# The second product of a feed-forward block in matmuls of 512 columns, with the 64 columns left over computed transposed

## The chip, the cores and the metric

The kernel runs on one core of a Trainium2 chip, in one launch. The metric is the time of an execution on the device in microseconds (us); three runs of the kernel before the change have a median of 1082.9 us (1082.35 to 1083.52). In the profile, PE is the matrix engine, PEld its weight loads, DVE the vector engine, ACT the scalar engine, POOL the third elementwise engine, and SP the queue that issues most DMAs.

## The reference, cut to what matters

```python
xn = _layernorm(x)                                    # x = A_q: 2048 rows, 576 columns
h  = jnp.maximum(jnp.einsum("bsd,df->bsf", xn, w1), 0)   # w1: 576 x 4608
B  = jnp.einsum("bsf,fd->bsd", h, w2)                 # w2: 4608 x 576: the second product
out = x + A(xn, k, v, shift_k, ssm_k, ssm_D) + B      # A: a causal long convolution with gates
```

A shifts and gates k and v, convolves them along the 2048 rows with ssm_k, and multiplies by xn. The kernel computes that convolution as matmul transforms of two steps (64 by 32).

## The kernel before, in words

All matmuls of the two products take fp32r operands, and every operand is split into a high part and a low part (`hi` by a rounding copy on ACT, `lo` by a subtraction on DVE or POOL), so that a product is the sum of three: high by high, high by low, low by high.

**Feed-forward.** The 2048 rows are 16 tiles of 128 rows (`T`), four blocks `b` of four tiles (`BT`). The 4608 hidden columns are 12 chunks `ci` of 384, each of three groups `j` of 128 (`FT`). The program passes twice over the 12 chunks (24 chunk visits), the first time with blocks 0 and 1, the second with blocks 2 and 3: 48 pairs of a chunk and a block. For each pair:

- `mm1` (line 334), three times: 14 matmuls of 512 columns (the moving operand is the transposed x of the block, `xhi`, `xlo`, `xhl`; the stationary one 128 by 128 of w1) into a PSUM tile `psh` of which there are two. ACT writes `hh` (the rectified high part, line 339), DVE `ll` (the low part, line 340).
- `mm2` (line 358), once for each of the four row tiles: for each half of the 576 output columns (`NH` = 288), nine matmuls of 288 columns, stationary a 128 by 128 slice of `hh` or `ll`, moving a half of `h2` or `l2` (high and low w2). The sum lies in a PSUM tile `pso`, of which there are three, and DVE adds it to `acc` in SBUF (line 362 for block 0, which is scaled by `rstd`, line 366 else).

That is 72 matmuls of 288 columns for a pair in `mm2`, 3456 in the program, beside 2016 of 512 columns in `mm1`. Every matmul has its own weight load of 128 by 128.

The weights of the next chunk are loaded by SP (`load_w1`, `load_w2`, lines 282 and 294) into single buffers, and split during the second block of a chunk: ACT writes the high part (lines 306 and 315), POOL the low part (line 277).

**Order.** `drain(n)` issues `mm2` tiles of the previous pair between the `mm1` groups of the next one: one after j=0, one after j=1, two after j=2. `tick(cost)` counts matmul columns and, at a rate from the totals, lets the generator `conv()` issue a further piece of the convolution: its matmuls are of 288 columns (lines 398, 562, 700 and 701) and stand in pairs or threes among those of the products, into the three PSUM tiles `psf`. A scheduler then sets the final order of the instructions on each engine. SP issues DMAs in order; in the first 60 us these are the loads of x, of the weights, and the many small pieces of `ssm_k` (`kt`, line 421).

At the end, the last row tile is stored in two halves, each issued by the SP and ACT queues after its addition (line 370).

## Time and profile before

| | |
|---|---|
| three runs, median | 1082.9 us (1082.35 to 1083.52) |
| span of the profiled execution (the page gives no time for it beside the span) | 1084.4 us |
| PE busy | 1070.8 us, 99% of the span |
| PEld busy | 977.2 us |
| DVE, ACT, POOL busy | 732.5, 585.0, 261.9 us |
| mean granted TensorE clock | 0.997 |
| matmuls | 6537: 2016 in `mm1`, 3456 in `mm2`, 960 in the convolution, 80 transposes, 25 to begin with |

The busy time of a matmul in the profile is from its start to its modelled end, and matmuls overlap. What a matmul costs in a full stream is the distance from its start to the start of the next one. The chain of waits gives this for whole stretches: a row such as "3.57 PE pso L358 x27" is 27 matmuls in a row that set the pace for 3.57 us. The timeline gives single starts.

### The profile page before, as it was taken

What the parts mean: (1) busy time and instruction counts of PE and PEld (TensorE: products, weight loads), DVE (VectorE), ACT (ScalarE), POOL (GpSimd) and SP (SyncE); (2) the same over time, 40 slices, a digit from 0 to 9 for tenths busy, and PEclk for the clock granted to TensorE, in tenths of its full rate; (3) what the DMA queues carried; (4) which work ended last, traced back from release to release, by engine and by line L of the source; (5) the groups of instructions that cost most, each with busy time, mean ns of one, the idle gap of its engine ahead of it and who ended that gap; (6) DMA issues with size and microseconds to landing.
All of it is one profiled execution on the core that took longest, in us unless ns stands there. A gap on an engine that the chain in (4) does not pass through costs nothing.

```text
span 1084.4 us, 17301 instructions
## 1 busy us (share of the span) xinstructions
PE 1070.8 (99%) x6537; PEld 977.2 (90%) x6537; DVE 732.5 (68%) x1213; ACT 585.0 (54%) x1184; POOL 261.9 (24%) x218
## 2 busy tenths in 40 slices
PE   8999999999999999999999999999999999999998
PEld 5889899998999999999999999899999999999998
DVE  5423677949998777677666676666656666876774
ACT  4221587823443323333388787888788864543430
POOL 4131222412312322312213031211113032332410
PEclk9999999999999999999999999999999999999999
DMA  9950345664644525325564343434344227745524
GB/s 217 181 145 27 119 147 190 195 185 133 187 138 136 153 77 164 117 60 171 190 182 135 99 135 99 135 99 136 92 143 141 80 103 221 201 130 143 164 81 110
DMA packets 112255, 150.79 MB, mean 139 GB/s; under 512 B 45261, under 2 KB 62927, under 8 KB 112172
## 3 DMA queue, kind: packets, MB, share of 16 engines
q1 hardware_dynamic: 103884, 135.50, 42.0%
q0 software_dynamic: 7968, 13.44, 4.8%
q8 instruction: 52, 0.85, 0.3%
q10 hardware_dynamic: 320, 0.74, 0.3%
q14 instruction: 31, 0.25, 0.1%
HBM read 114.26 MB, written 35.39 MB: 138 GB/s over the span
## 4 chain that ended last, share of the span: by engine, by line
PE 90%; DMA 4%; SPq 2%; DVE 2%; ACT 1%; issue 1%; POOL 0%; ACTq 0%; DVEq 0%
PE pso L358 40%; PE psh L334 39%; PE psf L562 7%; PE psf L398 3%; DMA r<-in_w 3%; SPq L421 2%; PE psf L700 1%; PE psf L701 1%; DMA k-1_2414<-in_k 1%; DMA sk<-in_shift_k 0%; PE psf L269 0%; DVE lok L553 0%; POOL l L277 0%; DVE k L611 0%; DVE lox L553 0%
## 5 line engine op out<-in xcount | busy, mean ns | idle before, releaser
L277 POOL TENSOR_TENSOR l<-r,h 128x640 fp32r<-128x640 f32 (+1 forms) x144 | 224.4, 1563 | 621.8 <-ACT h L306 448.3
L358 PE MATMUL pso<-h,hh 128*128 128x288 f32 x1152 | 337.3, 295 | 3.7 <-ACT hh L339 2.7
L358 PE MATMUL pso<-l,hh 128*128 128x288 f32 x1152 | 338.5, 295 | 0.0
L358 PE MATMUL pso<-h,ll 128*128 128x288 f32 x1152 | 337.7, 295 | 0.0
L334 PE MATMUL psh<-xhi,h 128*128 128x512 f32 x576 | 226.5, 394 | 1.1 <-DVE ll L340 1.1
L334 PE MATMUL psh<-xlo,h 128*128 128x512 f32 x576 | 226.5, 393 | 0.0
L334 PE MATMUL psh<-xhi,l 128*128 128x512 f32 x576 | 225.8, 392 | 0.0
L358 PEld LDWEIGHTS pso<-h,hh 128*128 128x128 f32 x1152 | 215.8, 188 | 10.4 <-ACT hh L339 3.4
L358 PEld LDWEIGHTS pso<-l,hh 128*128 128x128 f32 x1152 | 216.3, 188 | 5.8
L358 PEld LDWEIGHTS pso<-h,ll 128*128 128x128 f32 x1152 | 216.0, 188 | 0.6
L366 DVE TENSOR_TENSOR acc<-pso,acc 128x288 f32<-128x288 f32 x288 | 128.6, 451 | 75.1 <-PE pso L358 72.1
L339 ACT ACTIVATE hh<-psh 128x512 fp32r<-128x512 f32 x144 | 85.6, 595 | 169.1 <-PE psh L334 168.2
L340 DVE SCALAR_TENSOR_TENSOR ll<-psh,hh 128x512 fp32r<-128x512 f32 x144 | 99.0, 687 | 109.8 <-ACT hh L339 109.5
L334 PEld LDWEIGHTS psh<-xhi,l 128*128 128x128 f32 x576 | 108.4, 188 | 20.3
L334 PEld LDWEIGHTS psh<-xhi,h 128*128 128x128 f32 x576 | 108.4, 188 | 17.1 <-DVE ll L340 1.4
L334 PEld LDWEIGHTS psh<-xlo,h 128*128 128x128 f32 x576 | 108.6, 188 | 15.5 <-DVE xlo L204 0.4
L315 ACT ACTIVATE h<-r 128x576 fp32r<-128x576 f32 x72 | 48.9, 682 | 73.4 <-DMA r<-in_w 46.9
L362 DVE SCALAR_TENSOR_TENSOR acc<-pso,rstd,acc 128x288 f32<-128x288 f32 x96 | 48.3, 512 | 27.5 <-PE pso L358 26.5
L392 DVE TENSOR_TENSOR ks<-kt,ks 64x288 fp32r<-64x288 f32 x64 | 57.6, 901 | 3.3 <-ACT ks L391 1.3
L399 ACT ACTIVATE zx<-psf 128x288 f32<-128x288 f32 x64 | 25.8, 407 | 59.3 <-PE psf L398 38.9
L334 PE MATMUL psh<-xhl,l 128*128 128x512 f32 x144 | 56.4, 392 | 0.0
L334 PE MATMUL psh<-xhl,h 128*128 128x512 f32 x144 | 56.2, 391 | 0.0
(109 smaller groups left out, 1451.2 us busy)
## 6 DMA issues: line engine op xcount, KB each, us to landing
r<-in_w SPq DMA_DIRECT2D x24, 864.0 KB, 5.3
r<-in_w SPq DMA_DIRECT2D x23, 768.0 KB, 6.1
zk<-zk SPq DMA_DIRECT2D x32, 288.0 KB, 2.5
zx<-zx SPq DMA_DIRECT2D x32, 288.0 KB, 2.6
ztk<-zk SPq DMA_DIRECT2D x32, 288.0 KB, 3.0
ztx<-zx SPq DMA_DIRECT2D x32, 288.0 KB, 2.8
zy<-vo SPq DMA_DIRECT2D x32, 288.0 KB, 2.1
zo<-zy SPq DMA_DIRECT2D x32, 288.0 KB, 3.0
```

Of the source, the lines that this page charges most:

```text
L277: return nc.gpsimd.tensor_tensor(dst, src, hi, OP.subtract)
L315: nc.scalar.activation(h2, r2[:, j, :], AF.Copy)
L334: nc.tensor.matmul(ps, a, m, start=i == 0, stop=i == len(seq) - 1)
L339: done["act"] = nc.scalar.activation(hh, ps, AF.Relu)
L340: lows.append(nc.vector.scalar_tensor_tensor(ll, ps, 0.0, hh, op0=OP.max, op1=OP.subtract))
L358: nc.tensor.matmul(ps[:, :NH], a[:, cols], m[:, dc], start=n == 0, stop=n == 3 * FT - 1)
L362: done["acc"] = nc.vector.scalar_tensor_tensor(acc[t][:, dc], ps[:, :NH], rstd[:, t:t + 1], acc[t][:, dc], op0=OP.mult, op1=OP.add)
L366: done["acc"] = nc.vector.tensor_tensor(acc[t][:, dc], ps[:, :NH], acc[t][:, dc], OP.add)
L392: nc.vector.tensor_tensor(dst[other], src[own], dst[own], OP.subtract)
L398: nc.tensor.matmul(ps[:, :NH], w[:, u, n, :], stk, start=n == 0, stop=n == 1)
L399: nc.scalar.activation(z, ps[:, :NH], AF.Copy)
L562: nc.tensor.matmul(ps[:, :NH], a, m[:, cols], start=n == 0, stop=n == 2)
```

## The change

Output columns 0 to 511 of a row tile are now one PSUM tile with nine matmuls of 512 columns. The other 64 columns are computed once per pair for all four row tiles, transposed (`mm2_rest`): the stationary operand is a 128 by 128 piece of w2 with the high part of its last 64 columns beside their low part, the moving operand is `hh` and `ll` of the block (512 rows), six matmuls of 512 columns. The low part by low part is thereby added too. The two halves of the result, 64 partitions each, are summed over the chunks in an SBUF tile `accT`; after the last chunk of a pass, four transposes by PE bring them back, and DVE adds eight pieces of 128 by 64 to `acc`. For this, `h2` and `l2` become one tile `w` of 1152 columns, in the order: high 0 to 511, high 512 to 575, low 512 to 575, low 0 to 511; POOL writes the low part in two subtractions, of 512 and of 64 columns.

For a pair, 72 matmuls of 288 columns (20736 columns) become 36 + 6 of 512 (21504 columns). `drain` issues `mm2_rest` first, then the four tiles. `tick` is called once more for a pair, and in the middle of a tile's nine matmuls as well as behind them. The last row tile is added in two pieces of 256 columns after its nine matmuls, and stored in pieces of 256 and 320 columns.

```diff
-W_MM2 = FT * 6 * NH
+W_MM2 = FT * 3 * 512
+W_REST = FT * 2 * 512
+DM = 512
...
-FFN_TOTAL = NCHUNK * NB * (FT * W_MM1 + BT * W_MM2)
+FFN_TOTAL = NCHUNK * NB * (FT * W_MM1 + BT * W_MM2 + W_REST)
...
     def split_w2(ci, j):
         r2 = raw_w[2, ci]
-        h2 = wp.tile([P, D], F32R, tag="h2", name=f"h2_{ci}_{j}", bufs=2 * FT - 1)
-        l2 = wp.tile([P, D], F32R, tag="l2", name=f"l2_{ci}_{j}", bufs=2 * FT - 1)
+        w = wp.tile([P, 2 * D], F32R, tag="w2", name=f"w2_{ci}_{j}", bufs=2 * FT - 1)
         with at_turn(ci):
-            nc.scalar.activation(h2, r2[:, j, :], AF.Copy)
-        last = split_lo(l2, r2[:, j, :], h2)
+            nc.scalar.activation(w[:, :D], r2[:, j, :], AF.Copy)
+        split_lo(w[:, 2 * D - DM:], r2[:, j, :DM], w[:, :DM])
+        last = split_lo(w[:, D:2 * D - DM], r2[:, j, DM:], w[:, DM:D])
...
+    def mm2_rest(ci, b):
+        ps = ps_o.tile([P, 512], F32, tag="o", name=f"psr{ci}_{b}")
+        seq = [(weights[ci][j][2][:, DM:2 * D - DM], m) for j in range(FT) for m in hid[ci, b, j]]
+        for n, (a, m) in enumerate(seq):
+            nc.tensor.matmul(ps, a, m, start=n == 0, stop=n == len(seq) - 1)
+        if ci % NCHUNK == 0:
+            accT[b] = xp.tile([P, 512], F32, tag="accT", name=f"accT{b}")
+            done["acc"] = nc.vector.tensor_copy(accT[b], ps)
+        else:
+            done["acc"] = nc.vector.tensor_tensor(accT[b], ps, accT[b], OP.add)
+        tick(W_REST)
+        if ci % NCHUNK == NCHUNK - 1:
+            back = ps_o.tile([P, BT, 2, D - DM], F32, tag="o", name=f"psb{b}")
+            for i in range(BT):
+                nc.tensor.transpose(back[:, i], accT[b][:, i * P:(i + 1) * P], ident)
...
     def mm2(ci, b, i):
...
+        ps = ps_o.tile([P, 512], F32, tag="o", name=f"pso{ci}_{t}")
+        n = 0
+        for j in range(FT):
+            hh, ll = hid[ci, b, j]
+            w = weights[ci][j][2]
+            wh, wl = w[:, :DM], w[:, 2 * D - DM:]
+            for a, m in ((hh, wh), (hh, wl), (ll, wh)):
+                nc.tensor.matmul(ps, a[:, cols], m, start=n == 0, stop=n == 3 * FT - 1)
+                n += 1
+                if n == 5:
+                    tick(W_MM2 / 2)
+        last = ci == HALVES * NCHUNK - 1 and t == T - 1
+        for d in range(2) if last else range(1):
+            dc = slice(d * DM // 2, (d + 1) * DM // 2) if last else slice(0, DM)
...
-                    drain(1 if j < FT - 1 else BT)
+                    drain((2, 1, BT)[j])
```

In the changed program the lines of the products are 336 (`mm1`), 354 (`mm2_rest`), 364 (its transposes) and 388 (`mm2`). In the order of PE before, the 2016 matmuls of 512 columns stand in 292 unbroken stretches; in the changed order, 4032 of them stand in 348 unbroken stretches, broken by the convolution's matmuls of 288 columns and by transposes.

Three places in the order follow. In the names, the first number behind `pso` is the row tile, behind `psh`, `hh` and `ll` the block and the group j, behind `h`, `l` and `w` the chunk and the group; the last number is the scheduler's. The first place is PE's order near the first use of `hh_1_2` (block 1, group 2 of chunk 0). Before:

```order
L334 MATMUL psh_0_0_553<-xhl_137,l_1_0_417 128x512
L358 MATMUL pso_4_0_572<-h_0_1_231,ll_1_1_441 128x288
L358 MATMUL pso_4_1_584<-h_0_1_231,ll_1_1_441 128x288
L358 MATMUL pso_5_0_615<-h_0_0_227,ll_1_0_390 128x288
L358 MATMUL pso_5_0_615<-h_0_1_231,hh_1_1_440 128x288
L358 MATMUL pso_4_0_572<-h_0_2_235,hh_1_2_494 128x288
```

and now:

```order
L336 MATMUL psh_0_0_518<-xhl_137,l_1_0_415 128x512
L354 MATMUL psr_1_537<-ll_1_1_439,w_0_1_231 128x512
L354 MATMUL psr_1_537<-hh_1_2_481,w_0_2_235 128x512
L388 MATMUL pso_4_547<-w_0_1_231,ll_1_1_439 128x512
L388 MATMUL pso_4_547<-w_0_2_235,hh_1_2_481 128x512
```

The first use stands at the same place relative to `mm1`, but now in the matmuls of the 64 columns. Ahead of it, from the first matmul of `mm1` on, there were 98 matmuls of 512 columns and 88 of 288; now there are 154 of 512. The order of SP up to there is the same, and ACT writes `hh_1_2` right behind the same split of w2 (`h_1_0`, now `w_1_0`).

The second place is DVE's order near the first product of the shift convolution (`e_1`, which reads the DMA into `k-1`). Before:

```order
L340 SCALAR_TENSOR_TENSOR ll_0_1_2483<-psh_0_1_2467,hh_0_1_2482 128x512
L366 TENSOR_TENSOR acc_217<-pso_5_0_2486,acc_217 128x288
L366 TENSOR_TENSOR acc_217<-pso_5_1_2497,acc_217 128x288
L486 TENSOR_TENSOR e_1_2529<-k-1_2414,sk 128x576
L483 TENSOR_TENSOR c_2508<-k_2418,sk 128x576
L487 TENSOR_TENSOR c_2508<-c_2508,e_1_2529 128x576
L340 SCALAR_TENSOR_TENSOR ll_0_2_2533<-psh_0_2_2514,hh_0_2_2532 128x512
L366 TENSOR_TENSOR acc_220<-pso_6_0_2536,acc_220 128x288
```

and now:

```order
L342 SCALAR_TENSOR_TENSOR ll_0_1_2166<-psh_0_1_2147,hh_0_1_2165 128x512
L400 TENSOR_TENSOR acc_217<-pso_5_2169,acc_217 128x512
L342 SCALAR_TENSOR_TENSOR ll_0_2_2210<-psh_0_2_2187,hh_0_2_2209 128x512
L521 TENSOR_TENSOR e_1_2144<-k-1_2052,sk 128x576
L518 TENSOR_TENSOR c_2131<-k_2056,sk 128x576
L400 TENSOR_TENSOR acc_220<-pso_6_2213,acc_220 128x512
```

`e_1` moved behind the `ll` of one further `mm1` group, and each addition behind it frees a PSUM tile of 512 columns.

The third place is the end of PE's order. There was nothing but `mm2` in the last 108 matmuls; now the last block's six matmuls of the 64 columns and their transposes stand ahead of its four row tiles:

```order
L388 MATMUL pso_11_10421<-w_23_2_10089,ll_2_2_10239 128x512
L354 MATMUL psr_3_10434<-hh_3_0_10304,w_23_0_9951 128x512
L354 MATMUL psr_3_10434<-ll_3_0_10305,w_23_0_9951 128x512
L354 MATMUL psr_3_10434<-hh_3_1_10369,w_23_1_10011 128x512
L354 MATMUL psr_3_10434<-ll_3_1_10370,w_23_1_10011 128x512
L354 MATMUL psr_3_10434<-hh_3_2_10406,w_23_2_10089 128x512
L354 MATMUL psr_3_10434<-ll_3_2_10407,w_23_2_10089 128x512
L364 MATMUL psb_10442<-ident,accT_5194 128x128 x4
L388 MATMUL pso_12_10455<-w_23_0_9951,hh_3_0_10304 128x512 x2
```

The transposes read `accT_5194`, which DVE writes from `psr_3`, and nothing stands between the two on PE. At the other three such places (one for each block) 14 or more matmuls of `mm1` stand between them.

More of the change, by code (lines that the diff above doesn't have):

```diff
@@ L291, in load_w1 @@
         raw_w[1, ci] = r1
-        weights[ci] = [[None, None, None, None] for _ in range(FT)]
+        weights[ci] = [[None, None, None] for _ in range(FT)]
     def load_w2(ci):
@@ L311, in split_w2 @@
         r2 = raw_w[2, ci]
-        h2 = wp.tile([P, D], F32R, tag="h2", name=f"h2_{ci}_{j}", bufs=2 * FT - 1)
-        l2 = wp.tile([P, D], F32R, tag="l2", name=f"l2_{ci}_{j}", bufs=2 * FT - 1)
+        w = wp.tile([P, 2 * D], F32R, tag="w2", name=f"w2_{ci}_{j}", bufs=2 * FT - 1)
         with at_turn(ci):
-            nc.scalar.activation(h2, r2[:, j, :], AF.Copy)
-        last = split_lo(l2, r2[:, j, :], h2)
-        weights[ci][j][2:] = h2, l2
+            nc.scalar.activation(w[:, :D], r2[:, j, :], AF.Copy)
+        split_lo(w[:, 2 * D - DM:], r2[:, j, :DM], w[:, :DM])
+        last = split_lo(w[:, D:2 * D - DM], r2[:, j, DM:], w[:, DM:D])
+        weights[ci][j][2] = w
         return last
@@ L324, in mm1 @@
     def mm1(ci, b, j):
-        h1, l1, _, _ = weights[ci][j]
+        h1, l1, _ = weights[ci][j]
         hi, lo, hl = xT[b]
@@ L342, in mm1 @@
         hid[ci, b, j] = (hh, ll)
+    accT = {}
+    def mm2_rest(ci, b):
[13 more added lines that the diff above has]
+                nc.tensor.transpose(back[:, i], accT[b][:, i * P:(i + 1) * P], ident)
+            for i in range(BT):
+                t = b * BT + i
+                to = acc[t][:, DM:]
+                for n in range(2):
+                    if b == 0:
+                        done["acc"] = nc.vector.scalar_tensor_tensor(
+                            to, back[:, i, n], rstd[:, t:t + 1], to, op0=OP.mult, op1=OP.add)
+                    else:
+                        done["acc"] = nc.vector.tensor_tensor(to, back[:, i, n], to, OP.add)
     def mm2(ci, b, i):
@@ L349, in mm2 @@
                 next(stream)
-        for h in range(2):
-            ps = ps_o.tile([P, 512], F32, tag="o", name=f"pso{ci}_{t}_{h}")
-            dc = slice(h * NH, (h + 1) * NH)
-            n = 0
-            for j in range(FT):
-                hh, ll = hid[ci, b, j]
-                _, _, h2, l2 = weights[ci][j]
-                for a, m in ((hh, h2), (hh, l2), (ll, h2)):
-                    nc.tensor.matmul(ps[:, :NH], a[:, cols], m[:, dc],
-                                     start=n == 0, stop=n == 3 * FT - 1)
-                    n += 1
+        ps = ps_o.tile([P, 512], F32, tag="o", name=f"pso{ci}_{t}")
[12 more added lines that the diff above has]
+            dc = slice(d * DM // 2, (d + 1) * DM // 2) if last else slice(0, DM)
             if b == 0:
                 done["acc"] = nc.vector.scalar_tensor_tensor(
-                    acc[t][:, dc], ps[:, :NH], rstd[:, t:t + 1], acc[t][:, dc],
+                    acc[t][:, dc], ps[:, dc], rstd[:, t:t + 1], acc[t][:, dc],
                     op0=OP.mult, op1=OP.add)
             else:
-                done["acc"] = nc.vector.tensor_tensor(acc[t][:, dc], ps[:, :NH], acc[t][:, dc],
+                done["acc"] = nc.vector.tensor_tensor(acc[t][:, dc], ps[:, dc], acc[t][:, dc],
                                                       OP.add)
-            if ci == HALVES * NCHUNK - 1 and t == T - 1:
+            if last:
+                to = slice(dc.start, D if d else dc.stop)
                 for u, queue in ((0, nc.sync), (1, nc.scalar)):
-                    queue.dma_start(out[u, :, t, dc], acc[t][halves(u)[0], dc])
-            tick(W_MM2 / 2)
+                    queue.dma_start(out[u, :, t, to], acc[t][halves(u)[0], to])
+        tick(W_MM2 / 2)
         if ci % NCHUNK == NCHUNK - 1:
@@ L780, in drain @@
         for _ in range(n):
-            if done < BT:
-                mm2(ci, b, done)
-                done += 1
-        prev = (ci, b, done) if done < BT else None
+            if done == 0:
+                mm2_rest(ci, b)
+            elif done <= BT:
+                mm2(ci, b, done - 1)
+            done += 1
+        prev = (ci, b, done) if done <= BT else None
     for half in range(HALVES):
@@ L815, in h3_ffn_kernel @@
                         load_acc(t)
-    drain(BT)
+    drain(BT + 1)
     rest_of_stream()
```

## The prediction

> **What bounds the kernel now.** I read the page's busy times and its chain of waits first, then PE's waits, then the chain piece by piece.

> ```profile
> PE 1070.8 (99%) x6537; PEld 977.2 (90%) x6537; DVE 732.5 (68%) x1213; ACT 585.0 (54%) x1184; POOL 261.9 (24%) x218
> PE 90%; DMA 4%; SPq 2%; DVE 2%; ACT 1%; issue 1%; POOL 0%; ACTq 0%; DVEq 0%
> ```

> ```profile
> PE pso L358 <- ACT hh L339: 2.7, 2, 2.5
> PE psf L562 <- DVE k L598: 1.2, 2, 0.6
> PE pso L358 <- DVE acc L366: 0.9, 1, 0.9
> ```

> PE sets the end: 99% busy, 90% of the chain. It waited 2.7 us for `hh`, 0.9 us for an addition and 1.2 us in the convolution; other engines have room. So the change is worth what it changes in PE's stream, plus what it does to these few waits. A matmul's price is the distance between starts, not the busy 295 or 393 ns. The chain piece by piece (start, length, engine, tile, line, count) gives it:

> ```profile
> 60.81 1.59 PE psh L334 x7
> 62.40 0.65 PE pso L358 x5
> 63.05 0.69 PE psh L334 x3
> ...
> 64.94 2.53 PE psh L334 x11
> 67.47 3.57 PE pso L358 x27
> ...
> 102.58 3.18 PE psh L334 x14
> ```

> ```profile
> 297.32 3.23 PE psh L334 x14
> 1066.12 14.29 PE pso L358 x108
> ```

> The last 108 matmuls of 288 columns took 14.29 us, 132.3 ns each; 3.57 / 27 gives the same. With 512 columns the pieces differ: 3.23 / 14 is 231 ns, 3.18 / 14 is 227. Between 60.81 and 105.76 us there are 13 `psh` pieces with 105 matmuls in 24.05 us, 229.0 each. The longest stream of 512 columns alone shows the settled price:

> ```profile
> 17.19 0.39 PE L334 MATMUL psh<-xlo,h 128*128 128x512 f32 x1
> ...
> 21.27 0.39 PE L334 MATMUL psh<-xhl,l 128*128 128x512 f32 x1
> ```

> Eighteen distances lie between these starts: 4.08 / 18 = 226.7 ns. So I read a settled 226.7 ns and an extra that each stretch pays when it begins behind matmuls of another width: (24.05 - 105 x 0.2267) / 13 = 0.02 us a stretch.

> **The stream of PE.** Before, without its waits: 2016 x 0.2267 + 292 stretches x 0.02 + 3456 x 0.1323 = 457.0 + 5.8 + 457.2 = 920.0 us. Changed: 4032 x 0.2267 + 348 x 0.02 = 914.1 + 7.0 = 921.1 us. That is +1.1 us. Fewer matmuls pay for their fixed part, but there are 768 columns more in each of 48 pairs, and they nearly cancel: at the settled price alone, 42 x 226.7 = 9.52 us a pair against 72 x 132.3 = 9.53. The bounds are the cheapest and the dearest price seen: 226.7 (914.1 us, -5.9) and 230.7 (930.2 us, +10.2). I take the settled price with 0.02 us a stretch, because each convolution pair now interrupts a stream of 512 columns, where before it often stood among equals.

> [...]

> **The wait near 54 us.** The largest wait has a fixed end.

> ```profile
> 48.47 6.97 DMA r<-in_w
> ```

> ```profile
> 53.88 0.29 PE L358 MATMUL pso<-h,hh 128*128 128x288 f32 x1
> 55.47 0.68 ACT L315 ACTIVATE h<-r 128x576 fp32r<-128x576 f32 x1 [8.80 <-DMA r<-in_w]
> 56.05 0.58 ACT L339 ACTIVATE hh<-psh 128x512 fp32r<-128x512 f32 x1
> 56.69 0.61 PE L358 MATMUL pso<-h,hh 128*128 128x288 f32 x1 [2.51 <-ACT hh L339]
> ```

> ```profile
> 53.90:56.60 2.70, 0.28 (x3) 0.04 (x1) 0.00 (x0) 1.14 (x3) 0.38 (x1) 0.98 1.24 194
> 56.60:59.90 3.30, 3.21 (x10) 2.93 (x11) 2.11 (x4) 1.09 (x3) 2.42 (x2) 0.50 1.05 227
> ```

> The w2 load of chunk 1 lands at 55.4 us; ACT splits it, only then writes `hh_1_2`, and PE goes on at 56.69. (In the rows by stretch, the column behind POOL's is the granted clock: behind the idle stretch it is 0.50, which costs some 3.3 / 2 = 1.6 us more.) SP's and ACT's orders up to there are the same, so the wait ends at the same time. What counts is how much PE has done by then: before 98 x 0.2267 + 88 x 0.1323 = 33.86 us, changed 154 x 0.2267 = 34.91. So 1.05 us more work fits ahead of a wait that ends when it did: -1.05, and the +1.1 of the stream is down to about 0. Were this wait hidden altogether, 2.8 + 1.6 = 4.4 us would go; the 1.05 us are too little for that.

> [...]

> **What is added on PE.** Sixteen transposes.

> ```profile
> 507.01 1.03 PE L269 MATMUL psf<-ident,xn 128*128 128x128 f32 x8
> 507.80 0.52 PE L398 MATMUL psf<-xs,wx 128*128 128x288 f32 x2
> ```

> Eight took 0.79 us up to the next start, so sixteen take 1.6. Those of the last block wait for DVE with nothing between; for that and for the last addition these rows serve:

> ```profile
> L204 DVE TENSOR_TENSOR xlo<-psf,xhi 128x512 fp32r<-128x512 f32 x15 | 9.9, 685 | 5.0 <-ACT xhi L203 5.0
> L366 DVE TENSOR_TENSOR acc<-pso,acc 128x288 f32<-128x288 f32 x288 | 128.6, 451 | 75.1 <-PE pso L358 72.1
> ```

> ```profile
> 1079.97 1.41 SPq L370 DMA_DIRECT2D out<-acc  x2
> 1080.10 0.29 PE L358 MATMUL pso<-h,ll 128*128 128x288 f32 x1
> 1080.43 0.46 DVE L366 TENSOR_TENSOR acc<-pso,acc 128x288 f32<-128x288 f32 x1 [0.73 <-PE pso L358]
> ```

> DVE starts 0.04 us behind the end of a matmul (1080.10 + 0.29 to 1080.43). After the start of the last `psr` matmul come 0.39 us to its end, 0.04, 0.685 for an addition of 512 columns and some 0.05 back to PE: 1.17 us, less the 0.23 us of its own slot: +0.95 us of waiting. At the three other places at least 14 `mm1` matmuls, over 3 us, cover it; without them each would cost the same 0.95.

> **The tail.** Before, one addition of 0.45 us follows the last matmul, and the first half's store is already issued. Now two of 256 columns follow; by the two rows a column costs (685 - 451) / 224 = 1.04 ns, so 0.42 us each: +0.38. The two issues of SP take 1.41 us, 0.7 each; the second must now wait until the first, which begins with the first addition's end, is out: 0.7 - 0.42 = +0.28. Together +0.65 us.

> **The wait for an addition, and what changes off PE.**

> ```profile
> 235.84 0.46 DVE L366 TENSOR_TENSOR acc<-pso,acc 128x288 f32<-128x288 f32 x1 [1.38 <-PE pso L358]
> 241.66 0.76 DVE L486 TENSOR_TENSOR e<-k-1_2414,sk 128x576 f32<-128x576 f32 x1 [5.36 <-DMA k-1_2414<-in_k]
> ```

> DVE stood 5.36 us in front of `e`, which waits for a DMA; the additions behind it freed no PSUM tile, three tiles of 9 x 0.1323 = 1.19 us ran full, and PE lost 0.9 us. Now `e` stands one `mm1` group later and a tile lasts 9 x 0.2267 = 2.04 us: -0.9. It stays at 0 if the DMA is late by more than this adds. The 1.2 us in the convolution I leave as they are.

> DVE's additions cost the same: 4 x 0.685 + 0.685 = 3.4 us a pair against 8 x 0.451 = 3.6. The eight additions of 64 columns have no row; each lies between nothing and the 0.45 us of 288 columns, so at most 3.6 us. The third row tile behind the last transposes is the first to need their PSUM tile, 2 x 2.04 = 4.1 us on; without that cover it is up to 3.6 us. I take 0.

> ```profile
> L277 POOL TENSOR_TENSOR l<-r,h 128x640 fp32r<-128x640 f32 x72 | 116.5, 1619 | 452.8 <-ACT h L306 448.3 <-PE psf L562 4.5
> L277 POOL TENSOR_TENSOR l<-r,h 128x576 fp32r<-128x576 f32 x72 | 108.0, 1506 | 169.0 <-ACT h L315 168.8
> ```

> POOL's second subtraction for each split adds its fixed part: a column costs (1619 - 1506) / 64 = 1.77 ns, so about 1506 - 576 x 1.77 = 0.49 us stays, 35 us in 72 splits. POOL is busy for 262 of 1084 us and a split is first read about a block, over 20 us, later; without that cover it would be up to 0.5 us a split. `tick` comes 15 times a pair for 14, and its rate follows the new total: no term.

> **The sum:** +1.1 - 1.05 + 1.6 + 0.95 + 0.65 - 0.9 = +2.35 us. The page gives the profiled execution 1084.4 us of span and no time beside it; the median is 1082.9, 0.14% less. I put the difference on the median: **1085.2 us**, +0.2%.

> **Rivals.**

> - *The stream stays settled* (not slower). If a stretch behind another width pays nothing, 4032 x 0.2267 = 914.1 in place of 921.1: 1085.2 - 7.0 = 1078.2 us. It decides below a mean of 228.0 ns for 512 columns (then the time is no longer over 1082.9). For it: 3.18 / 14, and the 18 distances of 226.7. Against it: 3.23 / 14 in a stretch in the convolution. 0.17.
> - *It does not settle* (slower). All matmuls of 512 columns cost the 229.0 of the 105: 923.3, so +2.2: 1087.4 us; 230.7 would be 1094.3. For it: the stretches are short, 4032 / 348 = 11.6 on average. Against it: the 105 hold stretches just as short. 0.16.
> - *The clock does not fall near 54 us, or the convolution's waits go.* -1.6 or -1.2: 1083.6 to 1084.0. For it: the wait is 1 us shorter. Against it: the row with 0.50 behind 2.7 us. 0.12.
> - *Time goes by columns* (slower). If 288 columns had only been slowed by something else, and time followed the columns at 229.0 / 512 = 0.447 ns, 768 more in 48 pairs would cost 16.5 us: 1099.4 plus what is added. Against it: a column costs 0.459 ns at 288. 0.04. [...]
> - *A new wait*, for a PSUM tile that `psr` or `psb` holds: some 3 us, 1088. The three tiles now serve five groups of nine or six matmuls in a pair; each must be added within two more groups, 4.1 us, and an addition takes 0.69. 0.05.

> **Chances.** My forecast has 0.46, with a range of its own of 1083 to 1087.5. What a measurement of this kernel can tell from no change is about 0.2%, 2.2 us: slower is above 1085.1, faster below 1080.7. The forecast lies on that line: 0.23 same, 0.23 slower. The settled stream gives 0.14 faster and 0.03 same; the unsettled one 0.14 slower and 0.02 same; the shorter waits 0.02 faster and 0.10 same; columns and the new wait 0.09 slower. Faster 0.16, same 0.38, slower 0.46. The range goes from 1079.5, which takes in most of the settled stream, to 1090.0.

> **What would show it.** In the chain, stretches of 512 columns at 226.7 to 231 ns with a mean near 228.4; the same wait near 54 us, ending at 56.7, with a clock of 0.50 behind it; no wait for an addition near 243 us; a wait of about 1 us at the last transposes, at line 364; DVE's two last additions of 0.42 us. It is wrong if the mean of 512 columns is off by 1 ns (4 us), or if PE waits elsewhere for over 2 us.

## The result, and the profile after

The changed kernel takes 1101.4 us in the median (four runs, 1098.7 to 1103.1), beside 1083.2 us for the kernel before on the same chip: **1.0165 times as long, 95% interval 1.0149 to 1.018**, 18 us more. The forecast was 1085.2 with a range to 1090.0, so the prediction is wrong in size. Slower was its likeliest side, but the runs below show another reason than the forecast had.

The changed kernel's page first: busy times, and the chain by engine.

```profile
PE 1077.9 (98%) x5113; PEld 901.1 (82%) x5113; DVE 715.5 (65%) x1102; ACT 592.7 (54%) x1184; POOL 286.4 (26%) x290
PE 92%; DMA 3%; SPq 3%; DVE 1%; issue 1%; ACT 0%; POOL 0%; DVEq 0%; ACTq 0%
```

PE still sets the end. Its waits are others than before (who waited <- for whom: us in total, times, longest):

```profile
PE psf L735 <- DVE y L738: 6.2, 4, 3.2
PE psf L433 <- issue: 2.3, 1, 2.3
PE psr L354 <- ACT hh L341: 2.0, 3, 1.5
...
PE psb L364 <- DVE accT L359: 0.8, 1, 0.8
```

Lines 433 and 735 are matmuls of the convolution: 433 in its first two stages (`fk`, `fx`), 735 and 736 in the last (`fo`); its middle stage `fm` is line 597. Neither place stood in the prediction. The rows by stretch show what the larger one, at `fo`, costs: the changed kernel around the start of `fo` (us, then busy time and count of PE, PEld, DVE, ACT and POOL, then the granted clock, DMA share and GB/s).

```profile
932.00:941.00 9.00, 9.00 (x44) 7.58 (x43) 2.96 (x4) 2.66 (x4) 1.62 (x3) 1.00 0.86 241
941.00:959.00 18.00, 11.84 (x39) 9.33 (x38) 14.29 (x25) 11.07 (x23) 3.30 (x4) 0.62 0.87 266
959.00:968.00 9.00, 9.00 (x44) 7.50 (x43) 6.85 (x13) 4.23 (x10) 2.33 (x3) 1.00 0.29 85
```

In 18 us PE did 39 matmuls at a mean clock of 0.62; on either side it did 44 in 9 us. The kernel before, in the 18 us in which its own `fo` begins, lost nothing: PE was busy throughout at full clock (its 113 are more also because most are narrower).

```profile
905.00:923.00 18.00, 18.00 (x113) 16.58 (x113) 15.59 (x27) 10.15 (x21) 4.18 (x4) 1.00 0.87 255
```

PE's timeline and the chain there give the reason:

```profile
941.34 0.39 PE L336 MATMUL psh<-xhl,l 128*128 128x512 f32 x1
944.95 0.61 PE L735 MATMUL psf<-ohi,wi 128*128 128x288 f32 x1 [3.23 <-DVE y L738]
945.36 0.44 PE L736 MATMUL psf<-olo,wi 128*128 128x288 f32 x1
...
947.62 0.61 PE L735 MATMUL psf<-ohi,wi 128*128 128x288 f32 x1 [0.86 <-DVE y L738]
...
949.86 0.61 PE L735 MATMUL psf<-ohi,wi 128*128 128x288 f32 x1 [0.92 <-DVE y L738]
```

```profile
930.33 2.06 DMA zy<-vo
...
936.33 6.63 DMA zo<-zy
...
943.07 0.69 ACT ohi L691
943.78 0.76 DVE olo L692
944.54 0.37 DVE y L738
```

`fm` ends only at 929.5 us, `fo` begins with a read of what it stored, and in PE's order 18 `fo` matmuls stand together with no product between them. So PE waits for the load, then every few matmuls for ACT and DVE, which split the next rows and empty the PSUM tiles; and from 944.77 to 958.42 us the granted clock is 0.50, where 288 columns take 0.24 us (945.36 to 945.60) in place of 0.132. The profile shows both; that it is the bunching of the `fo` matmuls which makes the waits is tested by e3.

A balance of the whole of PE's stream follows from the distance of each matmul's start to the next. "Full price" counts 227, 132 and 109 ns for 512, 288 and 128 columns; "small" is what distances exceed it by up to 25 ns, "slow" what the longer ones exceed it by (us; the 1.2 us ahead of the first start are in no column):

| profiled run | full price | small | slow | after the last start | span |
|---|---|---|---|---|---|
| before | 1054.5 | 6.4 | 18.0 | 4.3 | 1084.4 |
| changed | 1057.6 | 6.6 | 26.5 | 5.0 | 1096.9 |

The slow distances added are 11.9 us at 941 to 958, 4.4 at 251 to 258 and 1.1 at the last transposes; gone are 2.7 before 45 us, 2.5 near 54, 1.2 near 243, 2.3 at 648 and 691 (two of the convolution's waits), and 0.5 near 122. The two profiled spans are 12.5 us apart, the medians 18.3. The changed kernel's profiled run is the fastest of its four, 2.8 us under their median. The span of the profile before, 1084.4, is above all four times of that kernel, 1082.4 to 1083.5, and in the other runs the time is about 1.8 us above the span, so by estimate that execution was some 3 us longer than the timed ones. Small places of one profile, above all near 54 us, are therefore not to be read as the difference of the medians (e9 and e10).

Where a wait's length is given in a sentence, it is the distance between two starts less the matmul's own price; the idle times in the fences are up to 0.2 us shorter.

Counted in PE's order, by the share of the products' columns issued so far, the convolution's stages stand thus:

| | `fx` | `fm` | `fo` | most `fo` matmuls together |
|---|---|---|---|---|
| before | 0.237 to 0.510 | 0.524 to 0.820 | 0.829 to 0.980 | 6 or fewer |
| changed | 0.234 to 0.509 | 0.525 to **0.857** | 0.868 to 0.975 | **18** |

### The profile page after: what moved, and what is told of

The parts are those of the page before. It is cut to its first block, busy times and chain, and to the rows that moved or that the text cites. A ratio compares the mean times of both kernels' runs of the same rounds, so it can differ in the third digit from the quotient of the medians.

```text
span 1096.9 us, 14552 instructions
## 1 busy us (share of the span) xinstructions
PE 1077.9 (98%) x5113; PEld 901.1 (82%) x5113; DVE 715.5 (65%) x1102; ACT 592.7 (54%) x1184; POOL 286.4 (26%) x290
## 4 chain that ended last, share of the span: by engine, by line
PE 92%; DMA 3%; SPq 3%; DVE 1%; issue 1%; ACT 0%; POOL 0%; DVEq 0%; ACTq 0%
PE psh L336 39%; PE pso L388 35%; PE psf L597 7%; PE psr L354 6%; PE psf L433 3%; DMA r<-in_w 2%; SPq L456 2%; PE psf L735 1%; PE psf L736 1%; DMA zo<-zy 1%; PE psf L271 0%; SPq L154 0%; DVE olo L692 0%; DVE y L738 0%; SPq L290 0%
## 5 line engine op out<-in xcount | busy, mean ns | idle before, releaser
L388 PE MATMUL pso<-w,hh 128*128 128x512 f32 x1152 | 365.5, 394 | 0.0
L388 PEld LDWEIGHTS pso<-w,hh 128*128 128x128 f32 x1152 | 213.4, 189 | 37.6
L279 POOL TENSOR_TENSOR l<-r,h 128x640 fp32r<-128x640 f32 x72 | 116.2, 1615 | 442.0 <-ACT h L308 439.1
L388 PE MATMUL pso<-w,ll 128*128 128x512 f32 x576 | 226.0, 393 | 0.0
L279 POOL TENSOR_TENSOR w<-r,w 128x512 fp32r<-128x512 f32 (+1 forms) x144 | 133.3, 949 | 142.1 <-ACT w L316 141.9
L400 DVE TENSOR_TENSOR acc<-pso,acc 128x512 f32<-128x512 f32 (+1 forms) x145 | 98.8, 683 | 48.7 <-PE pso L388 48.1
L388 PEld LDWEIGHTS pso<-w,ll 128*128 128x128 f32 x576 | 108.9, 189 | 20.3
L588 DVE TENSOR_TENSOR lok<-ztk,hik 128x576 fp32r<-128x576 f32 x32 | 25.3, 790 | 98.4 <-ACT hik L587 98.4
L316 ACT ACTIVATE w<-r 128x576 fp32r<-128x576 f32 x72 | 48.8, 682 | 52.9 <-DMA r<-in_w 42.5
L354 PE MATMUL psr<-hh,w 128*128 128x512 f32 x144 | 56.6, 393 | 2.0 <-ACT hh L341 2.0
```

The costliest lines, as they stand in the source:

```text
L279: return nc.gpsimd.tensor_tensor(dst, src, hi, OP.subtract)
L316: nc.scalar.activation(w[:, :D], r2[:, j, :], AF.Copy)
L354: nc.tensor.matmul(ps, a, m, start=n == 0, stop=n == len(seq) - 1)
L388: nc.tensor.matmul(ps, a[:, cols], m, start=n == 0, stop=n == 3 * FT - 1)
L400: done["acc"] = nc.vector.tensor_tensor(acc[t][:, dc], ps[:, dc], acc[t][:, dc], OP.add)
```

## The experiments

Theory A: the product is priced about rightly, and the rest is lost where the convolution's matmuls now stand. Theory B: the new product is itself dearer. In the table, ratios are to the kernel before on the same chip.

| run | edit | ratio (95%) |
|---|---|---|
| e1 | changed, PSUM tiles `pso` 2, `psf` 4 | 1.0164 (1.0144 to 1.0183) |
| e2 | before, the same | 1.0123 (1.0102 to 1.0143) |
| e4 | changed, product alone | 0.8716 (0.8703 to 0.8729) |
| e5 | before, product alone | 0.8777 (0.876 to 0.8794) |
| e3 | changed, `fo` later | 1.0054 (1.0037 to 1.007) |
| e6 | changed, `fx` later | 1.0147 (1.0131 to 1.0164) |
| e7 | changed, both later | 1.0032 (1.0011 to 1.0052) |
| e8 | before, `fo` later | 0.9997 (0.9985 to 1.001) |
| e9 | changed, `kt` loads behind the weights | 1.0113 (1.0098 to 1.0128) |
| e10 | before, the same | 0.9984 (0.9975 to 0.9993) |
| e11 | changed, e9 + e7 + transposes covered | 1.0043 (1.0027 to 1.006) |
| e12 | as e11, pauses of `fx` spread | 1.0032 (1.002 to 1.0045) |
| e13 | changed, 256 columns twice for 512 | 1.0238 (1.0221 to 1.0255) |
| e14 | as e12, `fo` in time | 0.9991 (0.9981 to 1.0002) |

### The product alone: e4 and e5

```diff
-    stream = conv()
+    stream = nothing()          # a generator that yields nothing
...
-                    nc.sync.dma_start(fin[t // 2], pairs[t - 1])
+                    move(pairs[t - 1], out, slice(t - 1, t + 1), store=True)
```

> The changed kernel without the convolution: its generator yields nothing, and the rows of the first half are stored without the convolution's part, so it computes the feed-forward block alone. To be read against e5. Theory A: e4 minus e5 is the price of the product's form alone, +1 to +5 us (16 transposes 1.6, the wait for the addition before them 0.8 to 1.0, the tail 0.65, the stream 1.1, less what waits go). Theory B: +14 to +18 us. By the rows of the profile (960 matmuls of the convolution at 0.132 us are gone, and its waits) both kernels come to 945 to 970 us.

> The kernel before without the convolution, in the same way as e4 (the feed-forward block alone): the other side of the pair. 945 to 968 us by both theories.

946.6 and 953.7 us: alone, the new form is **7.1 us faster**. Theory B falls, and A was too pessimistic as well. Both kernels here leave out the convolution. In the chain of the changed form alone, stretches run at the settled price (4.08 / 18 is 226.7 ns, 3.17 / 14 is 226.4):

```profile
60.92 4.08 PE pso L385 x18
71.58 3.17 PE psh L336 x14
```

Its products break off to another width 13 times; the form before does so 241 times even without the convolution, since its own halves of 288 columns stand among the 512 of `mm1`. That is "small" -1.9 against +4.5 us. The form before alone also loses 5.4 us near 483 to 496 us, where PE waits for the second pass's first rows, and 3.6 us more before 45 us:

```profile
PE psf L269 <- issue: 2.7, 1, 2.7
...
PE psh L334 <- DVE ll L340: 1.3, 1, 1.3
```

The profiled spans are 9.4 us apart (944.1 and 953.5; the second is the slowest of its four runs). The column "small" makes 6.4 us of that and "slow" 6.7, against +3.1 at full price and +0.7 at the end. So only about 2.6 us are the stream's own, and why the two waits go in the changed form stays open.

With the convolution beside it, its pairs break the stream in either form (292 and 347 times), "small" is 6.4 and 6.6 us, and this gain is not to be had.

### More PSUM for the convolution: e1 and e2

```diff
-    ps_o = ctx.enter_context(tc.tile_pool(name="ps_o", bufs=3, space=PSUM))
-    ps_f = ctx.enter_context(tc.tile_pool(name="ps_f", bufs=3, space=PSUM))
+    ps_o = ctx.enter_context(tc.tile_pool(name="ps_o", bufs=2, space=PSUM))
+    ps_f = ctx.enter_context(tc.tile_pool(name="ps_f", bufs=4, space=PSUM))
```

> The changed kernel with one edit: the PSUM pool of the products has 2 tiles for 3, that of the convolution's pieces 4 for 3. In the order of PE the convolution's middle stage (fm) then ends at 0.794 of the products' columns, for 0.857 in the changed kernel and 0.820 before, and the 18 matmuls of the last stage (fo) that stood together at 0.869 are spread. Theory A (order: the product itself costs 2 to 4 us more, and the rest of the 18 us is lost where the convolution's pieces now stand, about 13 us of it at 941 to 958 us where the fo run waits and the clock falls): 1084 to 1090 us. Theory B (the matmuls of the product are themselves dearer in the new form, by about 16 us in all): 1098 to 1102 us, no less. Theory C (two tiles are too few for the product): PE waits at lines 354 and 388 for the additions, 1095 us or more.

> The kernel before with the same edit of the two PSUM pools, as the control for e1: how much of e1 is the pools and not the change. Theory A: fm was only 0.013 late before (0.820 for an emission that ends at 0.807), so little is to be had: 1080 to 1087 us. Theory B says the same of this run; what B needs is that e1 minus e2 stays at 16 to 19 us, where A has it at 1 to 6 us.

Both times were missed: 1104.2 and 1099.0 us. The order came out as said and the slow distances at 941 us are gone, but the edit brings its own waits, in the kernel before as well. In e1 they are many short ones, some 17 us of slow distances between 245 and 1090 us where the changed kernel has 4.4 and 11.9 at its two places. The first row is of e1, the second of e2:

```profile
PE pso L388 <- DVE acc L396: 1.9, 1, 1.9
```

```profile
PE psf L562 <- ACT hix L552: 3.6, 1, 3.6
```

The edit costs the kernel before 13 us. What can be read is the difference, 5.2 us, inside A's 1 to 6 and far from B's 16 to 19; it is weak support, since each of the two runs has waits of its own. A repair by more tiles is no repair.

### The run of `fo` matmuls: e3, with e8 as its control

```diff
-            yield -PAUSE            # ahead of fo
+            yield -5 * PAUSE
...
-                    yield W_FO
+                    yield 0.75 * W_FO
```

> The changed kernel with the convolution's last stage (fo) alone written out later: five pauses for one ahead of it, and 0.75 of the weight for each of its pairs, so that the end stays in reach. In the order of PE the middle stage stays as late as in the changed kernel (its last matmul at 0.857 of the products' columns), but the 18 matmuls of fo that stood together are spread, and fo ends at 0.991 for 0.975. Theory A (the run of fo matmuls waits for their loads and for ACT and DVE, and the clock falls behind it: 11.9 us of slow distances at 941 to 958 us): 9 to 12 us less than the changed kernel, 1.004 to 1.008 times the kernel before. Theory D (not the run, but that the middle stage is late: loads of weights and of rows now fall together whatever the order): 1.013 or more. Theory E (fo now ends too late and the end waits for it): the gain at 941 us comes back behind 1060 us.

> The kernel before with the same edit of the fo stage as e3, as its control: it has no run of fo matmuls to be spread. Theory A: within 3 us of the kernel before (0.997 to 1.003). If the edit in itself gains (fewer loads at the same time, a shorter last stage), e8 falls by as much as e3 does against the changed kernel.

e3 is 1.0054 for 1.0165, inside A's 1.004 to 1.008: about **12 of the 18 us** lay in that run (each ratio is good to some 2 us). `fm` is as late as in the changed kernel, so its lateness costs nothing in itself (D falls), and no gain came back behind 1060 us (E falls). The stretch that was slow has, in e3, 88 matmuls for 39, and the full clock:

```profile
941.00:959.00 18.00, 18.00 (x88) 15.27 (x87) 13.06 (x21) 9.64 (x19) 4.99 (x4) 1.00 0.73 222
```

The same edit of the kernel before is worth nothing (0.9997).

### The start of `fx`: e6 and e7

```diff
                 tap(1, n)
                 yield -PAUSE / 8
+            yield -1 * PAUSE
```

> The changed kernel with one more pause ahead of the first matmuls of the convolution's second stage (fx) alone; the run of fo matmuls stays (22 together for 18). In the order of PE the first fx matmul moves from 0.2341 of the products' columns to 0.2374, where it is before (0.2372). Theory A (the second place: 4.4 us of slow distances at 251 to 258 us, a wait of 2.3 us for the split on DVE and the half clock behind it): that place is gone, the other stays, 3 to 5 us less than the changed kernel, 1.011 to 1.014 times the kernel before. If the wait has to do with DVE's work in the new form and not with where the matmul stands, it is back at the new place: 1.016.

> The changed kernel with both: the fo stage written out later and one more pause ahead of fx. Theory A: both places gone, 13 to 16 us less than the changed kernel, 0.999 to 1.004 times the kernel before. If the two places are not the cause but only where a loss that is fixed elsewhere shows, 1.010 or more.

In the changed kernel the second place is this: PE waits from 251.7 us while DVE never stands still, and behind it the granted clock is 0.50 from 255.28 to 258.69 us. The profile names no releaser ("issue"); PE goes on at 254.05, right behind the first half of DVE's `xs`, which is what I take it to wait for (`xs` are the split rows that the `fx` matmuls read).

```profile
251.50:254.00 2.50, 0.21 (x1) 0.00 (x0) 2.44 (x3) 0.00 (x0) 1.84 (x2) 1.00 0.81 224
254.00:258.50 4.50, 4.45 (x15) 3.51 (x16) 4.47 (x7) 1.72 (x4) 0.00 (x0) 0.64 0.00 0
```

e6 took that place away, and a wait for `xs` of 2.7 us came up at 305 us instead; its ratio of 1.0147 is not told apart from 1.0165, so A's forecast for e6 failed and the rival in its expectation is the one that was borne out. e7 has the wait too:

```profile
PE psf L433 <- DVE xs L427: 2.1, 1, 2.1
```

e7 comes to 1.0032, within what A gave, but 12 of its 14 us are those of e3, and the other 2 are within the noise. That moving `fx` gains anything is not shown. In the first 60 us of `fx`, DVE is full in both kernels (before, then changed):

```profile
260.00:320.00 60.00, 60.00 (x367) 54.97 (x366) 56.86 (x85) 23.66 (x45) 14.35 (x12) 1.00 0.48 145
```

```profile
260.00:320.00 60.00, 60.00 (x280) 50.22 (x279) 57.48 (x77) 24.29 (x46) 15.48 (x15) 1.00 0.53 162
```

So `xs` is late wherever DVE has a queue, and whether PE notices is a matter of where `xs` is first used. One thing that fills DVE's queue stands in DVE's rows around the wait at 251.7 us, and in POOL's beside the second of them:

```profile
248.30 1.85 DVE L521 TENSOR_TENSOR e<-k,sk 128x576 f32<-128x576 f32 x1
...
251.34 1.82 DVE L522 TENSOR_TENSOR c<-c,e 128x576 f32<-128x576 f32 x1
...
254.76 0.76 DVE L521 TENSOR_TENSOR e<-k-1_2052,sk 128x576 f32<-128x576 f32 x1
```

```profile
251.27 2.06 POOL L279 TENSOR_TENSOR w<-r,w 128x512 fp32r<-128x512 f32 x2 [0.94 <-ACT w L316]
```

An operation that takes 0.76 us took 1.8 beside a subtraction of POOL. Of the changed kernel's 128 operations of this kind (`e` and `c`), all 12 that took over 1.1 us overlap POOL's subtractions by 0.9 us or more, and the 90 that overlap none took at most 0.76. The two rows at 248.30 and 251.34 alone took 2.1 us longer, about as long as PE stood idle. No run moved POOL's work, so that the wait would go with it is not shown. Why the kernel before gets by without a wait there stays open: it has as little room on DVE, and 19 such slow operations.

### The wait near 54 us: e9 and e10

```diff
-                    nc.sync.dma_start(kt[halves(h)[0], d:d + KD, :], src)
+                    with tc.issue_after(done["w2"].ins):      # the load of chunk 1's w2
+                        nc.sync.dma_start(kt[halves(h)[0], d:d + KD, :], src)
```

> The changed kernel with the loads of the convolution's filter (kt, 16 of them on SP's queue) put behind the load of the second chunk's weights in the program, alone. In the order of SP the three loads of weights r_1 then stand ahead of all kt loads instead of behind 10 and 14 of them; the order of PE is left as it was. In five profiles so far (before, e1, e3, e6, e7) the wait of the second product for those weights near 53 us took 2.3 to 5.0 us, and with the half clock behind it 4.1 to 6.5 us of slow distances; in the profiled run of the changed kernel, its fastest, 1.6 and 1.8. Theory F (the wait ends with that load, and its length varies from run to run): the place is gone, 3 to 5 us less than the median of the changed kernel, 1.011 to 1.014 times the kernel before, and the spread between runs shrinks. Rival: the wait is one of the weights' own path (ACT and POOL split them) and stays, 1.016.

> The kernel before with the same edit of the kt loads as e9, as its control. Theory F: its place at 54 us (4.2 us of slow distances) is gone as well, 3 to 5 us less, 0.995 to 0.997 times the kernel before. Rival: no change.

SP's queue in e7, where it is as in the changed kernel (start, us, what it issued, how many): the small pieces of `kt` keep it busy for 24 us ahead of the weights.

```profile
12.88 24.33 SPq L456 DMA_DIRECT2D kt<-in_ssm_k  x10
37.39 1.65 SPq L290 DMA_DIRECT2D r<-in_w  x1
...
48.30 1.55 SPq L299 DMA_DIRECT2D r<-in_w  x1
```

In e9:

```profile
18.49 0.40 SPq L290 DMA_DIRECT2D r<-in_w  x1
...
23.08 0.40 SPq L299 DMA_DIRECT2D r<-in_w  x1
23.53 13.38 SPq L457 DMA_DIRECT2D kt<-in_ssm_k  x6
```

The last of these weights are issued 25 us earlier, the wait is gone, and by the ratios e9 lies about 5.6 us under the changed kernel, with four runs within 1.1 us (4.4 before). This wait, 1.6 us in one profiled run and up to 5.0 in another, is thus one thing that sets the runs apart; it is not the only one, since the runs of e10, e11 and e12, which do not have it, lie 3.4 to 6.0 us apart. e10 gained less than forecast: its profiled span is 4.1 us shorter, its median only 1.8. Why the edit is worth so much less there stays open.

### All places mended: e11, e12 and e14

e11 joins the edits of e9 and e7, and writes the transposes behind the first row tile of the last block; e12 and e14 replace the one pause ahead of `fx` by four halves and lower the convolution's total share (`SHARE`) from 0.985 to 0.965 and 0.94; e14 has seven pauses ahead of `fo` and half its weight for each pair.

```diff
-        if ci % NCHUNK == NCHUNK - 1:          # in mm2_rest
-            back = ...
+    def back_to_rows(ci, b):                   # called behind mm2(ci, b, 0)
+        if ci % NCHUNK == NCHUNK - 1:
+            back = ...
...
+            yield -PAUSE / 2                   # e12, e14: ahead of fx, and
+                if t < 3:                      # behind its row blocks 0 to 2
+                    yield -PAUSE / 2
```

> The changed kernel with four edits together: the kt loads behind the weights (e9), fo written out later (e3), one more pause ahead of fx (e6), and in the last block of each half the transposes written behind the first row tile's matmuls, so that the addition before them is covered. Worked out from e7 (1.0032 times the kernel before): less 4.8 us of the place at 54 us and less 0.9 us of the wait before the transposes: 0.997 to 0.999 times the kernel before. What stays is the wait for the split at the start of fx (3.9 us in e7). If the fo stage, which now ends at 0.998 of the columns, holds up the end, 1.003 or more.

> As e11, but in place of the one pause ahead of fx four halves of a pause: one ahead and one behind each of its first three row blocks, with a total share of 0.965 for 0.985 so that the convolution still ends in reach. If PE's wait at the start of fx is one for a DVE that is full there (28 to 29.6 us busy in each 30 us from 260 to 320 us), the spread takes it away: 3 to 4 us less than e11, 0.993 to 0.996 times the kernel before. If it only moves to another row block, as it did from 251 us to 305 us in e6 and e7, e12 comes out with e11.

> As e12 (kt loads behind the weights, four half pauses spread over the first row blocks of fx, fo later, the addition before the transposes covered), with a total share of 0.94 for 0.965, seven pauses for five ahead of fo and half its weight per pair: in the order of PE fo then ends at 0.991 of the products' columns for 0.998. If what is lost is only in the places, the tail of 9.3 us of e11 and e12 goes back to 5.0 and the rest stays: 0.997 to 1.000 times the kernel before. If the loss returns at another place whenever one is mended, 1.003 or more.

e11 missed its 0.997 to 0.999: its slow distances fell to 10.9 us, but `fo` ended at 0.998 of the columns and held up the end, as its last clause had it. After the last matmul's start the span goes on for 9.3 us in e11 and e12, where it is 5.0 in the changed kernel. The spread of e12 did not do what it was to do: the wait for `xs` of 1.7 us at 299 us in e11 stands as 1.5 us at 252 us in e12, and the two ratios overlap. e14, with `fo` in time, is **0.9991**: the loss is gone and nothing is won. Its waits:

```profile
PE psf L435 <- issue: 1.4, 1, 1.4
...
PE psf L271 <- issue: 0.9, 1, 0.9
PE psr L354 <- ACT hh L341: 0.6, 2, 0.3
```

Beside e10, the kernel before with the same wait mended, the balance is full price 1057.6 against 1054.5, small 6.6 against 6.4, slow 13.8 against 13.9, end 5.0 against 4.3: **+3.9 us of span** for the new product in these two profiles, once the places are mended in both. By the ratios, 0.9991 and 0.9984, it is only 0.8 us, and the two intervals overlap; e14's profiled run is 1.2 us above its median and e10's 0.4 below, on another chip. So the new product costs some 1 to 4 us, and the runs do not say more closely. Among the versions that do all the work, only e10 has its interval below the kernel before; it gains 0.16%.

### What moved the order: e13

```diff
-            for a, m in ((hh, wh), (hh, wl), (ll, wh)):
-                nc.tensor.matmul(ps, a[:, cols], m, start=n == 0, stop=n == 3 * FT - 1)
+        for q in (slice(0, 256), slice(256, 512)):
...
+                for a, m in ((hh, wh), (hh, wl), (ll, wh)):
+                    nc.tensor.matmul(ps[:, q], a[:, cols], m[:, q], start=n == 0, stop=n == 3 * FT - 1)
```

> The changed kernel with each matmul of 512 columns of a row tile written as two of 256 into the same PSUM tile (first 9 for the left half, then 9 for the right); tiles, additions, transposes and the number of steps of the convolution as in the changed kernel. In the order of PE the middle stage ends at 0.800 of the products' columns (0.857 in the changed kernel, 0.820 before) and the run of 18 fo matmuls is gone. On the chip by that: no wait and no half clock at 941 to 958 us, 11.9 us of slow distances less. The price of the width: on the line through 132.3 ns for 288 columns and 226.7 ns for 512 a matmul of 256 takes 118.8 ns, two of them 10.9 ns more than one of 512, 1728 times: 18.8 us; so 1.018 to 1.026 times the kernel before. If time goes by columns alone (113.4 ns), the width costs nothing and it is 1.002 to 1.006. If the place is one of the tiles and additions of the new form, it is still there: 1.030 or more.

The step in the middle of a tile now stands between its two halves; by the program's counters `fm` and `fo` are written out where they were. The run gives 1.0238, inside the forecast. `fm` ends at 0.800 in PE's order, the slow distances at 941 us are gone, and the width costs what the line gave: 8.64 / 72 is 120 ns for 256 columns.

```profile
1096.26 8.64 PE pso L389 x72
```

So it is the width of the product's matmuls, and with it their number, and not its tiles, additions or steps, that moved the convolution. As I read it, the scheduler lays out the order from its own account of time, in which the convolution's chain in `fm` is held by three `psf` tiles and spans more of the products' columns when these come in fewer, wider matmuls; that a fourth `psf` tile (e1) also brings `fm` forward, to 0.794, fits this. The reading is argued; no run shows the scheduler's account.

## Why the prediction was wrong, point by point

- **The step that failed** is the last sentence on what changes off PE, "`tick` comes 15 times a pair for 14, and its rate follows the new total: no term", with "the 1.2 us in the convolution I leave as they are". The steps at which pieces are written out did keep their pace (by the program's counters `fo` begins at 0.81 of the columns, 0.82 before); the order that the scheduler makes of them did not, and I had compared it at three places of the products only. The runs showed in its place: `fm` ends at 0.857 of the columns for 0.820, 18 `fo` matmuls stand together, and that costs 11.9 us of slow distances (12 us by e3, nothing by its control e8). The trace adds +4.4 at `fx`, less 2.8 at 122, 648 and 691 us; that the `fx` part would go with the order is not shown (e6). The other 6 of the 18 us the runs do not split cleanly between `fx`, the wait near 54 us and the product itself. The forecast's own sign of being wrong was met: PE waited elsewhere for over 2 us, 6.2 at line 735 and 2.3 at 433.
- **The stream, +1.1.** Right. Counted from the table: +3.1 at full price, of which 1.7 are the transposes, and +0.2 small: +1.6. The mean distance of 512 columns, without those over 252 ns, is 228.9 ns, where the forecast had 228.4. The line through the prices of the rows, 132.3 ns for 288 columns and 226.7 for 512, held too: it gives 118.8 ns for 256, and e13 has 120.
- **Transposes 1.6, their wait 0.95, tail 0.65.** Right to 0.2 or so: 16 x 0.109 = 1.7 at full price (1.4 by the starts, since the last of each four takes 0.03); the first of the last four starts 1.17 us behind the last `psr` matmul, 0.94 more than that one's own slot; 0.7. The chain at the end of the changed kernel:

```profile
1081.32 1.37 PE psr L354 x6
1082.69 0.02 issue
1082.71 0.70 DVE accT L359
1083.41 0.04 issue
1083.46 0.66 PE psb L364 x4
1084.12 8.20 PE pso L388 x36
```

- **The wait near 54 us, -1.05.** That the wait ends with the load was right (e9), the fixed end was not: the wait ended at 53.9 us in place of 56.7, and its length varies from run to run by more than the term. In the profiled run it was 1.6 us with the clock at 1.00 behind it, a gain of 2.5; in e3, e6 and e7 it was 2.3, 5.0 and 3.1 with the half clock (4.1 to 6.5 us of slow distances at this place in these three, e1 and the kernel before). By the ratios the edit that removes it is worth 5.6 us to the changed kernel and 1.7 to the one before, so in the median the place cost the changed kernel more, not 1.05 less.
- **The wait for an addition, -0.9.** Right; no wait stands near 243 us.
- **The rivals.** "Time goes by columns" gave 1099.4, closest to what was measured, and is refuted by e4 and e5, and by e13, whose 256 columns took 120 ns where it had 113.4: a right number from a wrong cause. "A new wait" was the right kind, at 0.05 far too low, and was looked for at the products' PSUM tiles and sized at 3 us. "The stream stays settled" is true where no convolution interrupts (e4), and only there.
- **The sum.** Between the profiled runs of e14 and e10 the product's form costs 3.9 us of span, by the ratios 0.8. The forecast's terms for what stays there, 1.1 + 1.6 + 0.65, make 3.35, which the traces bear out and the ratios do not. That the forecast had "slower" on its likeliest side was in part luck: the 18 us come mostly from a place that it gave no term.

## What to carry to other kernels

Where a second stream of work is woven into the one that sets the end, a change to the first moves the second: before pricing a single matmul, compare where every stage of the other stream begins, ends and bunches in the new order, above all where a stage reads what the one before has just stored. Then price the change with the other stream taken out and again with its places mended; here the change came to +18 us as first written, -7 with the other stream out, and some +1 to +4 with its places mended, mostly by pauses. Here the gain from long unbroken stretches ("small" at -1.9 us for +4.5 with the other stream out) was not there when that stream broke them (6.6 us for 6.4).

## What the runs showed of the hardware

```profile
251.87:255.28 3.41, 1.23 (x7) 1.05 (x8) 3.32 (x4) 0.70 (x2) 1.47 (x2) 1.00 0.48 123
255.28:258.69 3.41, 3.41 (x10) 2.64 (x9) 3.41 (x6) 1.03 (x3) 0.00 (x0) 0.50 0.00 0
258.69:262.10 3.41, 3.41 (x17) 2.81 (x17) 3.34 (x6) 1.65 (x3) 0.27 (x1) 1.00 0.45 143
...
941.36:944.77 3.41, 0.37 (x2) 0.00 (x0) 0.99 (x2) 1.66 (x4) 0.00 (x0) 1.00 1.05 318
944.77:958.42 13.65, 10.53 (x32) 8.53 (x33) 12.72 (x24) 8.83 (x19) 2.72 (x4) 0.50 0.82 252
```

In e6 a wait with 2.6 us of idle time, longer than the 2.3 at 251 us, lay across two such stretches, left PE 2.53 and 1.73 us busy in them, and cost no clock (1.00 up to 312 us):

```profile
303.11:306.52 3.41, 2.53 (x12) 1.77 (x10) 3.38 (x6) 1.09 (x2) 0.55 (x1) 1.00 0.56 150
306.52:309.93 3.41, 1.73 (x8) 1.50 (x9) 3.32 (x6) 1.89 (x5) 0.00 (x0) 1.00 0.78 263
```

In the kernel before, the steps ahead of its two with 0.50 had PE busy for 1.20 us (8.68 to 12.10 us) and 1.11 us (53.06 to 56.47 us). In the changed kernel the step with most of the wait near 54 us (50.48 to 53.89 us) had PE busy for 1.98 us, and the clock behind it was 1.00. How long the half clock lasted differed too: from 944.77 to 955.01 us PE was busy for 2.38, 2.09 and 2.65 us of each of three steps and the clock stayed at 0.50; it came back to 1.00 behind the next step, in which PE was busy throughout, as it was in the one step at 255.28 us.

**A change of width had a price.** In the changed kernel the first two distances of 512 columns behind another width are 232.8 ns in the mean, the third 229.7, the fourth 228.2; from the tenth on they are 226.7, and the last one ahead of a matmul of 288 columns is 235 to 237 in 264 of 330 cases.
